# Queries and keys turned on the host, and a new order of small steps, in a bucketed-attention and expert kernel on one core

## The chip, the core and the metric

The program runs on one core of a Trainium2 chip. Its time is device microseconds of one execution, here the median of three timed runs. Engines: PE (matmul, with PEld its weight loads), DVE (vector), ACT (scalar), POOL (general), and SP, which here only issues DMAs.

## The reference

```python
# 2 batches, 8 heads, 768 tokens, head size 64; 6 hash bits
q_bits = (np.einsum('bhsd,dk->bhsk', q, proj) > 0)        # k_bits likewise
mask = q_bucket[:, :, :, None] == k_bucket[:, :, None, :]  # bits as one number
scores = np.where(mask, scale * q @ k.T, -1e9)
attn = softmax(scores); out = attn @ v
# then per token: argmax expert of 8 (w_gate), a 512-1024-512 relu layer, scaled by two gates
# then a dense 512-2048-512 layer with ELU
```

## The kernel before

The work has three stages: attention (to about 246 us of the profile), the experts, the dense layer. Only the first is touched.

Attention goes over 16 heads in 8 pairs; a pair is one q, one k and one v load. A tile is 128 queries of one head against its 768 keys; 6 tiles a head, 12 a pair, 96 in all. Every fp32 value is held as a high part (fp32r) and a low part (the rest), so that two single-speed products stand for one.

The loop `for n in range(NQ + 3)` writes a software pipeline out by hand. Iteration n issues, in this order: the maximum of tile n-1 (`stage_M`: DVE, then two tiny POOL instructions that make `sc` and `bi`), POOL additions (`stage_A`), work put off from the iteration before (`early`), the transposes of tile n-3 (`stage_T`: six on PE into two PSUM buffers; ACT copies each to the high part `pthi`, DVE subtracts for the low part `ptlo`), the scores of tile n (`stage_S`: four matmuls), the router product of an older head (`stage_R`), four matmuls with V for tiles further back (`stage_V`), the exponential of tile n-1 (`stage_E`, ACT), and the evacuation of finished outputs (`stage_O`). Scores have two PSUM buffers `s`, so the scores of tile n+1 wait for the exponential of tile n-1. Transposes, the hash product `zps` and the router product share three PSUM buffers `t`. All engines run in order; SP issues all operand moves in one queue.

While a pair is computed, the next one is prepared. Four steps (`prep_T`: q and k, two halves each) take three PE transposes of the raw rows, an ACT copy to the high part and a DVE subtraction to the low part; two steps (`prep_Z`) take four matmuls with the hash weights, an ACT copy and a DVE comparison. `late` spreads them over the tiles: the PE part stands at the end of iteration s = 1, 2, 4, 5 (transposes) and 7, 8 (hash) of a pair's twelve, its ACT and DVE part in the next iteration, the copy ahead of that iteration's scores and exponential. `restack` then has SP move the halves by DMA into operand tiles `qa`, `qb`, `ka`, `kb` of the two heads; there are two sets of operand tiles, for the even and the odd pairs. The scores are a product over 128 rows (`a`: high and low parts) and one over 102 rows (`b`: 64 rows of a low part and, from row 64 on, hash bits and constants).

Of the kernel before, what the change touches and what calls it, by code (L numbers as in the profile page):

```python
# [8 lines left out]
F32 = mybir.dt.float32  # L9
# [11 lines left out]
NBITS = 6  # L21
MROWS = 32 + NBITS


@with_exitstack
def kernel(
# [94 lines left out]
    def load_pair(pr, what="qkv"):  # L121
        b, h0 = divmod(2 * pr, H)
        for src, nm in ((q, "q"), (k, "k"), (v, "v")):
            if nm not in what:
                continue
            if nm == "v":
                t = ap2.tile([128, 2, NC * D], F32, tag="raw_v", name="raw_v")
                nc.sync.dma_start(t, src[b, h0:h0 + 2].rearrange("h (p c) d -> p h (c d)", c=NC))
            else:
                t = ap2.tile([128, NC, 2 * D], F32, tag="raw_" + nm, name="raw_" + nm, bufs=2 if nm == "q" else 1)  # L130
                step = HALF if pr == 0 else NC
                for c0 in range(0, NC, step):
                    for hh in range(2):
                        nc.sync.dma_start(
                            t[:, c0:c0 + step, hh * D:(hh + 1) * D],
                            src[b, h0 + hh].rearrange("(p c) d -> p c d", c=NC)[:, c0:c0 + step],
                        )
            raw[pr, nm] = t
# [24 lines left out]
    def constant_rows(st, parts):  # L163
        for i, c0, c1 in parts:
            nm, p0, n, a = (("qb", 64, 32, 0.0), ("qb", 96, NBITS, -0.5), ("kb", 64, 32, -0.5))[i]
            nc.gpsimd.memset(opnd[st, nm][p0:p0 + n, c0:c1].bitcast(F32), a)

    constant_rows(1, [(i, 0, S) for i in range(3)])
    constant_rows(2, [(i, 0, S) for i in range(2)])
    amp = ap1.tile([128, 1], F32, name="amp")  # L170
    thr = ap1.tile([128, 1], F32, name="thr")
    for p0, n, a, t in (
        (0, 32, 0.0, -3e38), (0, 2 * NBITS, 1.0, 0.0), (32, 32, -0.5, -3e38),
        (64, 32, -0.5, -3e38), (64, NBITS, 1.0, 0.0), (96, 32, 1.0, 0.0),
    ):
        nc.vector.memset(amp[p0:p0 + n], a)
        nc.vector.memset(thr[p0:p0 + n], t)
# [4 lines left out]
    for hh in range(2):  # L182
        rows = slice(64 * hh, 64 * hh + 64)
        src = pj[rows, None, :].to_broadcast([64, 2, NBITS])
        for nm, g0, c0, step in ((0, 32 * hh, 0, NBITS), (1, 64, NBITS * hh, 32)):
            dst = bdf[rows, nm, g0:g0 + 2 * step].rearrange("p (r c) -> p r c", r=2)[:, :, c0:c0 + NBITS]
            nc.scalar.activation(dst, src, AF.Copy)
# [16 lines left out]
    def prep_T(pr, nm, j):  # L204
# [3 lines left out]
        r = raw[pr, nm]  # L208
        ps = prep_psum("prep")
        for c in range(HALF):  # L210
            cc = HALF * j + c
            nc.tensor.transpose(ps[:, c * 128:(c + 1) * 128], r[:, cc, :], ident)
        sl = slice(j * HC, (j + 1) * HC)
        sc = 1.0 / float(D) ** 0.5 / UNIT

# [3 lines left out]
        def evac_lo():  # L219
            if nm == "q":  # L220
                nc.vector.scalar_tensor_tensor(lo[:, sl], ps, sc, hi[:, sl], ALU.mult, ALU.subtract)
            else:
                nc.vector.tensor_tensor(lo[:, sl], ps, hi[:, sl], ALU.subtract)
            if j == 1 and pr:
                restack(pr, nm)

# [36 lines left out]
    def bit_weights():  # L263
        nc.gpsimd.memset(zwf, 0.0)
        for hh in range(2):
            rows = slice(64 * hh, 64 * hh + 64)
            for i, c0, r in ((0, 2 * NBITS * hh, 2), (1, 32 + NBITS * hh, 1)):
                dst = zwf[rows, i, c0:c0 + r * NBITS].rearrange("p (r c) -> p r c", r=r)
                nc.gpsimd.tensor_copy(dst, pj[rows, None, :].to_broadcast([64, r, NBITS]))
        nc.gpsimd.tensor_copy(zw[:, :, 0:64], zwf)  # L270
        nc.gpsimd.tensor_tensor(zw[:, :, 64:128], zw[:, :, 0:64], zwf, ALU.subtract)

    def prep_Z(pr, j):
# [12 lines left out]
        def compare():  # L286
            nc.vector.tensor_tensor(zt[pr][0:64, sl], ps[0:64], zb, ALU.is_gt)
            if j == 1:
                restack(pr, "z")

        early.append(compare)
        return (lambda: None), (lambda: None)

    def restack(pr, what, heads=(0, 1)):
        for hh in heads:
# [87 lines left out]

    def stage_T(n, between=None):
        m, i = divmod(n, HALF)
# [6 lines left out]
        for g in range(2):  # L392
# [316 lines left out]
    for n, st, i in ((1, 2, 2), (2, 3, 0), (6, 3, 1), (7, 3, 2)):  # L709
        for j in range(2):  # L710
# [240 lines left out]
    for n in range(NQ + 3):  # L951
# [489 lines left out]
```

## Time and profile before

| | us |
|---|---|
| median of three timed runs | 712.71 (712.57 to 713.49) |
| the profiled execution | 713.77 |
| span of its instructions | 712.0 |

PE is busy 98% of the span, DVE 78%, ACT 60%, POOL 30%. The granted TensorE clock is 1.00 in every stretch of the attention stage. A busy PE is not a PE at its peak, since matmuls overlap and their ends are modelled, so the distances between starts are read below rather than the busy share.

### The profile page before, as it was taken

What the parts mean: (1) busy time and instruction counts of PE and PEld (TensorE: products, weight loads), DVE (VectorE), ACT (ScalarE), POOL (GpSimd) and SP (SyncE); (2) the same over time, 40 slices, a digit from 0 to 9 for tenths busy, and PEclk for the clock granted to TensorE, in tenths of its full rate; (3) what the DMA queues carried; (4) which work ended last, traced back from release to release, by engine and by line L of the source; (5) the groups of instructions that cost most, each with busy time, mean ns of one, the idle gap of its engine ahead of it and who ended that gap; (6) DMA issues with size and microseconds to landing.
All of it is one profiled execution on the core that took longest, in us unless ns stands there. A gap on an engine that the chain in (4) does not pass through costs nothing.

```text
span 712.0 us, 12226 instructions
## 1 busy us (share of the span) xinstructions
PE 698.5 (98%) x4211; PEld 626.8 (88%) x4212; DVE 553.7 (78%) x1046; ACT 428.4 (60%) x855; POOL 211.1 (30%) x508
## 2 busy tenths in 40 slices
PE   8999999999999999999999999999999999999996
PEld 6899999999998988999999998788888888888884
DVE  6989898899998997788888887877788547934433
ACT  6988888888888865666666665445443224422221
POOL 7665445455456661221065311000000000002012
PEclk9999999999999999999999999999999999999998
DMA  8857758686691239788878986322222000001011
GB/s 188 198 136 178 186 129 210 163 189 164 144 233 57 84 116 299 239 261 242 261 209 247 256 217 144 104 88 75 89 87 92 2 0 1 0 1 60 0 60 62
DMA packets 108596, 97.39 MB, mean 137 GB/s; under 512 B 33480, under 2 KB 94728, under 8 KB 108528
## 3 DMA queue, kind: packets, MB, share of 16 engines
q1 hardware_dynamic: 106064, 90.15, 47.3%
q0 software_dynamic: 2304, 6.40, 2.4%
q8 instruction: 35, 0.57, 0.3%
q14 instruction: 33, 0.27, 0.1%
q10 hardware_dynamic: 160, 0.00, 0.0%
HBM read 64.15 MB, written 10.72 MB: 105 GB/s over the span
## 4 chain that ended last, share of the span: by engine, by line
issue 32%; PE 23%; DMA 6%; POOL 1%; ACT 0%; SPq 0%; POOLq 0%; ACTq 0%
PE hps L1135 11%; PE yps L1148 7%; DMA out_dram<-part,tidt 5%; PE yps L1150 3%; DMA xs<-xs_d 1%; PE xTp L1117 1%; DMA tidt<-tid_d 1%; PE yps L1147 0%; POOL xs L857 0%; POOL out_dram L1293 0%; ACT sum L1153 0%; POOL spacer L612 0%; SPq L743 0%; POOLq L1293 0%; ACTq L1153 0%
## 5 line engine op out<-in xcount | busy, mean ns | idle before, releaser
L399 DVE TENSOR_TENSOR ptlo<-t,pthi 128x384 fp32r<-128x384 f32 x192 | 99.9, 548 | 14.7 <-ACT pthi L398 13.1
L376 ACT ACTIVATE p<-s,bi,sc 128x768 f32<-128x768 f32 x96 | 95.9, 999 | 17.5 <-POOL bi L369 15.7
L832 DVE TENSOR_TENSOR wl<-wraw,wh 128x1024 fp32r<-128x1024 f32 (+1 forms) x65 | 77.4, 1194 | 23.7 <-ACT wh L828 21.4
L367 DVE TENSOR_REDUCE nm<-s 128x1 f32<-128x768 f32 x96 | 90.9, 947 | 0.3 <-PE s L349 0.3
L398 ACT ACTIVATE pthi<-t 128x384 fp32r<-128x384 f32 x192 | 84.8, 497 | 10.2 <-PE t L396 8.9
L1293 POOL DMA_INDIRECT out_dram<-part,tidt x12 | 11.5, 960 | 263.5 <-DVE part L1290 262.2
L1255 ACT ACTIVATE ee<-gps 128x512 f32<-128x512 f32 x48 | 28.7, 597 | 98.0 <-PE gps L1245 98.0
L1148 PE MATMUL yps<-h,wh 128*128 128x448 f32 x256 | 84.4, 380 | 0.0
L396 PE MATMUL t<-ident,p 128*128 128x128 f32 x576 | 79.5, 273 | 0.0
L1245 PE MATMUL gps<-x2h,vl 128*128 128x512 f32 x192 | 75.9, 395 | 0.0
L1275 PE MATMUL a<-vh,gh 128*128 128x512 f32 x192 | 75.6, 394 | 0.0
L1275 PE MATMUL a<-vh,gl 128*128 128x512 f32 x192 | 75.4, 393 | 0.0
L1245 PE MATMUL gps<-x2h,vh 128*128 128x512 f32 x192 | 75.3, 392 | 0.0
L1245 PE MATMUL gps<-x2l,vh 128*128 128x512 f32 x192 | 75.2, 392 | 0.0
L1275 PE MATMUL a<-vl,gh 128*128 128x512 f32 x192 | 74.9, 390 | 0.0
L349 PE MATMUL s<-ka,qa 128*128 128x384 f32 x192 | 73.4, 383 | 1.2 <-DMA qa<-qlo 0.4
L1258 ACT ACTIVATE gh<-ee 128x512 fp32r<-128x512 f32 x48 | 30.4, 633 | 69.2 <-DVE ee L1257 69.2
L1256 DVE TENSOR_SCALAR ee<-ee 128x512 f32<-128x512 f32 x48 | 20.4, 426 | 66.3 <-ACT ee L1255 66.2
L396 PEld LDWEIGHTS t<-ident,p 128*128 128x128 f32 x576 | 67.4, 140 | 3.9 <-DVE ptlo L399 0.5
L828 ACT ACTIVATE wh<-wraw 128x1024 fp32r<-128x1024 f32 x63 | 66.2, 1052 | 2.7 <-DMA wraw<-in_moe_w_dram 2.7
L413 PE MATMUL o<-pthi,vst 128*128 128x384 f32 x192 | 66.9, 349 | 0.3
L349 PE MATMUL s<-kb,qb 102*128 102x384 f32 x192 | 65.3, 341 | 0.4 <-DMA kb<-z 0.4
(224 smaller groups left out, 1768.8 us busy)
## 6 DMA issues: line engine op xcount, KB each, us to landing
wraw<-in_moe_w_dram SPq DMA_DIRECT2D x64, 512.0 KB
w<-in_moe_w_in_dram SPq DMA_DIRECT2D x16, 512.0 KB
w<-in_moe_w_out_dram SPq DMA_DIRECT2D x16, 512.0 KB
ka<-khi SPq DMA_DIRECT2D x30, 192.0 KB
xs_d<-zt SPq DMA_DIRECT2D x8, 528.0 KB
xs<-xs_d SPq DMA_DIRECT2D x8, 528.0 KB
raw_v<-in_v_dram SPq DMA_DIRECT2D x8, 384.0 KB
kb<-klo SPq DMA_DIRECT2D x15, 192.0 KB
```

The lines of the kernel that those rows point to most:

```text
L349: nc.tensor.matmul(ps[:, j, 0:HC], opnd[st, "q" + x][0:n1, cb], opnd[st, "k" + x][0:n1, j * HC:(j + 1) * HC], start=(x == "a"), stop=(x == ...
L367: nc.vector.tensor_reduce(nm, sps[n][:, :, 0:HC], AX.XY, ALU.max, negate=True)
L376: nc.scalar.activation(p.rearrange("p (a b) -> p a b", a=2), sps.pop(n)[:, :, 0:HC], AF.Exp, bias=bi, scale=sc, accum_out=sums[hd][:, c:c ...
L396: nc.tensor.transpose(ps[:, a, :], p[:, kt * 128:(kt + 1) * 128], ident)
L398: nc.scalar.activation(ho, ps, AF.Copy)
L399: nc.vector.tensor_tensor(lo[:, HALF * g:HALF * (g + 1), i * 128:(i + 1) * 128], ps, ho, ALU.subtract)
L413: nc.tensor.matmul(ops[m], vst[hd][:, kt, :], t[:, kt, :], start=(kt == 0 and x == 0), stop=(kt == NC - 1 and x == 1))
L832: fs = [lambda c=slice(j, j + h): eng.tensor_tensor(lo[:, c], r[:, c], hi[:, c], ALU.subtract) for j in range(0, PW, h)]
L1135: nc.tensor.matmul(ps, w[:, dc, fs], x[:, dc], start=(i == 0), stop=(i == len(terms) - 1))
L1148: nc.tensor.matmul(ps, wh[:, f], h[:, :, f], start=(f == 0), stop=last)
L1245: nc.tensor.matmul(ps, w[:, dc], x[:, dc, th * TC:(th + 1) * TC], start=(dc == 0 and i == 0), stop=(dc == KD - 1 and i == 2),)
L1275: nc.tensor.matmul(ps, x[:, cs], w, start=(fb in first_fb and i == 0), stop=(fb in last_fb and i == 2))
```

## The change

The host hands over q and k a second time, laid out as [batch, head, 64, 768] with the tokens in the order in which the transposes left them (`q_t`, `k_t`). Pairs 1 to 7 load these, one DMA each, in place of two loads of 256-byte runs, and `prep_T` reads them from SBUF: no PE transposes and no PSUM buffer for 28 steps. Pair 0 is as it was.

The order changes too. In a tile's transposes the second of two low parts is issued in the next iteration, behind that iteration's maximum. The preparation's ACT copies stand behind the exponential, its subtractions an iteration later at `early`. The steps stand at other tiles of the pair that is computed meanwhile (one tile ahead of it, then s = 0, 3, 5; hash steps at 4 and 8). `stage_R` comes a tile later for all but the last twelve tiles. `restack` moves k and the hash bits head by head, and the bits in four moves a pair in place of six; the `b` product has 82 rows in place of 102, with the constants placed anew. The diff, cut to its core (the constants' memsets, weights' columns and the list of inputs are left out):

```diff
     def load_pair(pr, what="qkv"):
+            elif pr:
+                t = ap2.tile([128, S], F32, tag="raw_" + nm, name="raw_" + nm, bufs=2 if nm == "q" else 1)
+                src = q_t if nm == "q" else k_t
+                nc.sync.dma_start(t, src[b, h0:h0 + 2].rearrange("h d s -> (h d) s"))
...
     def prep_T(pr, nm, j):
-        ps = prep_psum("prep")
-        for c in range(HALF):
-            cc = HALF * j + c
-            nc.tensor.transpose(ps[:, c * 128:(c + 1) * 128], r[:, cc, :], ident)
         sl = slice(j * HC, (j + 1) * HC)
+        if pr:
+            ps = r[:, sl]
+        else:
+            ps = prep_psum("prep")
+            for c in range(HALF):
+                cc = HALF * j + c
+                nc.tensor.transpose(ps[:, c * 128:(c + 1) * 128], r[:, cc, :], ident)
...
             if j == 1 and pr:
-                restack(pr, nm)
+                restack(pr, nm, (0, 1) if nm == "q" else (0,))
...
     def prep_Z(pr, j):
...
             if j == 1:
-                restack(pr, "z")
+                restack(pr, "z", (0,))
+                restack(pr, "k", (1,))
+                restack(pr, "z", (1,))
...
     def restack(pr, what, heads=(0, 1)):
...
-                k0 = 32 + NBITS * hh if pr else 64 + NBITS * hh
-                cp("kb", 64, zt[pr], k0, NBITS)
-                cp("kb", 96, zt[pr], k0, NBITS)
-                cp("qb", 64, zt[pr], 2 * NBITS * hh if pr else 32 * hh, 2 * NBITS)
+                q0, k0 = (2 * NBITS * hh, 32 + 2 * NBITS * hh) if pr else (32, 96)
+                cp("qb", 64, zt[pr], q0, 2 * NBITS)
+                cp("kb", 64 + NBITS, zt[pr], k0, 2 * NBITS)
...
-    def stage_T(n, between=None):
+    lows_t = []
+
+    def stage_T(n, later, between=None):
...
-            nc.vector.tensor_tensor(lo[:, HALF * g:HALF * (g + 1), i * 128:(i + 1) * 128], ps, ho, ALU.subtract)
+            po = lo[:, HALF * g:HALF * (g + 1), i * 128:(i + 1) * 128]
+            if g and later:
+                lows_t.append(lambda: nc.vector.tensor_tensor(po, ps, ho, ALU.subtract))
+            else:
+                nc.vector.tensor_tensor(po, ps, ho, ALU.subtract)
...
-    def prep(pr, i):
-        return prep_T(pr, "qqkk"[i], i % 2) if i < 4 else prep_Z(pr, i - 4)
+    highs = []
+
+    def prep(pr, nm, j):
+        high, low = prep_T(pr, nm, j)
+        highs.append(high)
+        early.append(lambda: early.append(low))
...
+    for p in range(1, NPAIR):
+        n0 = 2 * NC * (p - 1)
+        for n, nm, j in (
+            ((2, "q", 0), (3, "q", 1), (4, "k", 0), (5, "k", 1)) if p == 1
+            else ((-1, "q", 0), (0, "k", 0), (3, "q", 1), (5, "k", 1))
+        ):
+            at(n0 + n, prep, p, nm, j)
+        for j, n in enumerate((7, 8) if p == 1 else (4, 8)):
+            at(n0 + n, prep_Z, p, j)
...
         if 1 <= n < NQ + 1:
             stage_M(n - 1)
+        both(lows_t)
+        lows_t.clear()
         stage_A(n)
...
-        if late:
-            late[0]()
...
-        m, part = divmod(n - 13, HALF)
+        m, part = divmod(n - (14 if n < NQ - 12 else 13), HALF)
         if 0 <= m < NM - 3 and part == 0:
             early.append(stage_R(m))
...
         if 1 <= n < NQ + 1:
             stage_E(n - 1)
+        both(highs)
+        highs.clear()
...
-        if late:
-            late[1]()
-            late = []
...
+        if name.endswith("_t"):
+            a = inputs[name[:-2]]
+            b, h, t, d = a.shape
+            a = a.reshape(b, h, 128, t // 128, d).transpose(0, 1, 4, 3, 2).reshape(b, h, d, t)
```

DVE in pair 3's stretch, where pair 4 is prepared: `nm` is a tile's maximum, `ptlo` a low part of transposed weights, `qlo` and `klo` those of the next pair's preparation. Before:

```order
L399 TENSOR_TENSOR ptlo<-t,pthi 128x3x128 x2
L367 TENSOR_REDUCE nm<-s 128x1
L399 TENSOR_TENSOR ptlo<-t,pthi 128x3x128
L460 RECIPROCAL ri<-sm 128x3
L399 TENSOR_TENSOR ptlo<-t,pthi 128x3x128
L221 SCALAR_TENSOR_TENSOR qlo<-prep,qhi 128x384
L367 TENSOR_REDUCE nm<-s 128x1
L399 TENSOR_TENSOR ptlo<-t,pthi 128x3x128 x2
L221 SCALAR_TENSOR_TENSOR qlo<-prep,qhi 128x384
```

Now (L409 is the put-off second low part, L411 the first):

```order
L373 TENSOR_REDUCE nm<-s 128x1
L409 TENSOR_TENSOR ptlo<-t,pthi 128x3x128
L226 SCALAR_TENSOR_TENSOR qlo<-raw_q,qhi 128x384
L411 TENSOR_TENSOR ptlo<-t,pthi 128x3x128
L373 TENSOR_REDUCE nm<-s 128x1
L409 TENSOR_TENSOR ptlo<-t,pthi 128x3x128
L228 TENSOR_TENSOR klo<-raw_k,khi 128x384
L411 TENSOR_TENSOR ptlo<-t,pthi 128x3x128
L472 RECIPROCAL ri<-sm 128x3
L373 TENSOR_REDUCE nm<-s 128x1
```

A maximum that stood behind both low parts and a preparation's subtraction now stands behind the first low part alone; the subtraction stands behind the maximum and reads `raw_q` or `raw_k`, where it read the PSUM tile `prep`.

SP, the end of pair 1's stretch, where pair 2's operands (head 0: `qa_128` to `kb_131`; head 1: `_132` to `_135`) and pair 3's raw rows are moved. Before:

```order
L134 DMA raw_q<-in_q_dram 128x6x64 x2
L134 DMA raw_k<-in_k_dram 128x6x64 x2
L443 DMA o_1082<-o_1081 64x384
L300 DMA kb_131<-z 6x768 x2
L300 DMA qb_129<-z 12x768
L300 DMA kb_135<-z 6x768 x2
L300 DMA qb_133<-z 12x768
```

Now:

```order
L134 DMA raw_q<-in_q_t_dram 128x768
L307 DMA ka_130<-khi 64x768 x2
L307 DMA kb_131<-klo 64x768
L455 DMA o_1026<-o_1025 64x384
L134 DMA raw_k<-in_k_t_dram 128x768
L307 DMA qb_129<-z 12x768
L307 DMA kb_131<-z 12x768
L307 DMA ka_134<-khi 64x768 x2
L307 DMA kb_135<-klo 64x768
L307 DMA qb_133<-z 12x768
L307 DMA kb_135<-z 12x768
```

Head 0's bits were behind both raw loads and both heads' keys; now they are behind one load of k in one piece, and head 1's keys follow them.

## Rows read from the trace of the kernel before

**Rows 1.** The page's first part: busy us, share, instructions.

```profile
PE 698.5 (98%) x4211; PEld 626.8 (88%) x4212; DVE 553.7 (78%) x1046; ACT 428.4 (60%) x855; POOL 211.1 (30%) x508
```

**Rows 2.** Windows of pair 3 and pair 7; stretch, length, busy by engine.

```profile
96.50:126.29 29.79, 29.79 (x204) 28.85 (x202) 26.85 (x51) 26.13 (x59) 14.80 (x46) 1.00 0.68 173
...
216.75:246.02 29.27, 28.81 (x189) 26.77 (x188) 26.17 (x52) 24.90 (x55) 18.05 (x48) 1.00 0.22 79
```

**Rows 3.** Windows of four tiles: plain, with transposes, hash, router.

```profile
119.26:121.33 2.07, 2.07 (x18) 2.03 (x15) 1.93 (x4) 2.00 (x6) 1.01 (x4) 1.00 0.94 189
130.80:133.20 2.40, 2.40 (x20) 2.36 (x19) 1.92 (x5) 2.40 (x6) 1.44 (x3) 1.00 0.12 43
116.48:119.26 2.78, 2.78 (x22) 2.74 (x20) 2.46 (x5) 2.72 (x7) 0.91 (x3) 1.00 1.02 224
121.33:124.22 2.89, 2.89 (x24) 2.85 (x22) 2.89 (x6) 1.96 (x5) 1.70 (x7) 1.00 0.50 121
```

**Rows 4.** PE's timeline: start, length, instruction, at a preparation's transposes.

```profile
129.90 0.49 PE L212 MATMUL prep<-ident,raw_q 128*128 128x128 f32 x3
130.22 0.82 PE L396 MATMUL t<-ident,p 128*128 128x128 f32 x6
```

**Rows 5.** The timeline of a plain tile, all engines.

```profile
126.82 1.02 DVE L399 TENSOR_TENSOR ptlo<-t,pthi 128x384 fp32r<-128x384 f32 x2 [0.18 <-ACT pthi L398]
126.90 0.34 PE L349 MATMUL s<-kb,qb 102*128 102x384 f32 x1
...
127.75 0.95 DVE L367 TENSOR_REDUCE nm<-s 128x1 f32<-128x768 f32 x1
...
129.18 0.19 POOL L369 TENSOR_TENSOR bi<-sc,nm 128x1 f32<-128x1 f32 x1
...
129.40 0.99 ACT L376 ACTIVATE p<-s,bi,sc 128x768 f32<-128x768 f32 x1 [0.22 <-DVE ptlo L399]
...
130.80 0.42 PE L349 MATMUL s<-ka,qa 128*128 128x384 f32 x1
```

**Rows 6.** Waits over the span: total us, times, longest.

```profile
PEld s L349 <- ACT p L376: 5.0, 18, 0.5
...
PEld prep L212 <- DVE ptlo L399: 0.8, 2, 0.5
...
PE s L349 <- DMA kb<-z: 0.4, 1, 0.4
```

**Rows 7.** Groups by line and form: copies and subtractions from PSUM and SBUF.

```profile
L1259 DVE TENSOR_TENSOR gl<-ee,gh 128x512 fp32r<-128x512 f32 x48 | 33.1, 689 | 14.3 <-ACT gh L1258 13.3
L1258 ACT ACTIVATE gh<-ee 128x512 fp32r<-128x512 f32 x48 | 30.4, 633 | 69.2 <-DVE ee L1257 69.2
...
L1290 DVE TENSOR_TENSOR part<-a,part 128x512 f32<-128x512 f32 x24 | 15.6, 682 | 3.0 <-PE a L1275 3.0
...
L1288 ACT ACTIVATE part<-a 128x512 f32<-128x512 f32 x12 | 6.2, 595 | 0.0
```

**Rows 8.** ACT's timeline in a tile with a preparation's copy.

```profile
130.75 0.87 ACT L398 ACTIVATE pthi<-t 128x384 fp32r<-128x384 f32 x2 [0.27 <-PE t L396]
131.51 0.50 ACT L217 ACTIVATE qhi<-prep 128x384 fp32r<-128x384 f32 x1
131.88 1.00 ACT L376 ACTIVATE p<-s,bi,sc 128x768 f32<-128x768 f32 x1
132.76 0.22 ACT L376 ACTIVATION_READ_ACCUMULATOR p<-s,bi,sc 128x1 f32 x1
```

**Rows 9.** The expert stage: line 857 in all, then POOL's and DVE's timeline.

```profile
L857 POOL TENSOR_SCALAR xs<-xs x16: 1556/1798/3191, 248.0 to 406.0; 128x512 f32<-128x512 f32 x16
...
292.06 4.94 POOL L857 TENSOR_SCALAR xs<-xs 128x512 f32<-128x512 f32 x2 [13.01 <-DMA xs<-xs_d]
...
291.75 1.22 DVE L832 TENSOR_TENSOR wl<-wraw,wh 128x1024 fp32r<-128x1024 f32 x1 [0.49 <-ACT wh L828]
...
294.43 1.23 DVE L832 TENSOR_TENSOR wl<-wraw,wh 128x1024 fp32r<-128x1024 f32 x1 [0.56 <-PE hps L1135]
```

More of the change, by code (lines that the diff above doesn't have):

```diff
@@ L21 @@
 NBITS = 6
-MROWS = 32 + NBITS
+MROWS = 3 * NBITS
 @with_exitstack
@@ L38 @@
     w_out: bass.AP,
+    q_t: bass.AP,
+    k_t: bass.AP,
     out: bass.AP,
@@ L128, in load_pair @@
                 nc.sync.dma_start(t, src[b, h0:h0 + 2].rearrange("h (p c) d -> p h (c d)", c=NC))
+            elif pr:
+                t = ap2.tile([128, S], F32, tag="raw_" + nm, name="raw_" + nm, bufs=2 if nm == "q" else 1)
+                src = q_t if nm == "q" else k_t
+                nc.sync.dma_start(t, src[b, h0:h0 + 2].rearrange("h d s -> (h d) s"))
             else:
                 t = ap2.tile([128, NC, 2 * D], F32, tag="raw_" + nm, name="raw_" + nm, bufs=2 if nm == "q" else 1)
-                step = HALF if pr == 0 else NC
-                for c0 in range(0, NC, step):
+                for c0 in range(0, NC, HALF):
                     for hh in range(2):
                         nc.sync.dma_start(
-                            t[:, c0:c0 + step, hh * D:(hh + 1) * D],
-                            src[b, h0 + hh].rearrange("(p c) d -> p c d", c=NC)[:, c0:c0 + step],
+                            t[:, c0:c0 + HALF, hh * D:(hh + 1) * D],
+                            src[b, h0 + hh].rearrange("(p c) d -> p c d", c=NC)[:, c0:c0 + HALF],
                         )
@@ L164, in constant_rows @@
         for i, c0, c1 in parts:
[L165 to L169, printed above, removed]
+            nc.gpsimd.memset(opnd[st, ("qb", "kb")[i]][64:96, c0:c1].bitcast(F32), -0.5)
+    constant_rows(1, [(i, 0, S) for i in range(2)])
     amp = ap1.tile([128, 1], F32, name="amp")
@@ L172 @@
     for p0, n, a, t in (
-        (0, 32, 0.0, -3e38), (0, 2 * NBITS, 1.0, 0.0), (32, 32, -0.5, -3e38),
-        (64, 32, -0.5, -3e38), (64, NBITS, 1.0, 0.0), (96, 32, 1.0, 0.0),
+        (0, 32, -0.5, -3e38), (0, 2 * NBITS, 1.0, 0.0), (64, 32, 1.0, 0.0), (64, NBITS, -0.5, -3e38),
     ):
@@ L184 @@
         src = pj[rows, None, :].to_broadcast([64, 2, NBITS])
-        for nm, g0, c0, step in ((0, 32 * hh, 0, NBITS), (1, 64, NBITS * hh, 32)):
-            dst = bdf[rows, nm, g0:g0 + 2 * step].rearrange("p (r c) -> p r c", r=2)[:, :, c0:c0 + NBITS]
+        for i, c0 in ((0, 32 * hh), (1, 64 + (32 if hh else NBITS))):
+            dst = bdf[rows, i, c0:c0 + 2 * NBITS].rearrange("p (r c) -> p r c", r=2)
             nc.scalar.activation(dst, src, AF.Copy)
@@ L266, in bit_weights @@
             rows = slice(64 * hh, 64 * hh + 64)
-            for i, c0, r in ((0, 2 * NBITS * hh, 2), (1, 32 + NBITS * hh, 1)):
-                dst = zwf[rows, i, c0:c0 + r * NBITS].rearrange("p (r c) -> p r c", r=r)
-                nc.gpsimd.tensor_copy(dst, pj[rows, None, :].to_broadcast([64, r, NBITS]))
+            for i in range(2):
+                c0 = 32 * i + 2 * NBITS * hh
+                dst = zwf[rows, i, c0:c0 + 2 * NBITS].rearrange("p (r c) -> p r c", r=2)
+                nc.gpsimd.tensor_copy(dst, pj[rows, None, :].to_broadcast([64, 2, NBITS]))
         nc.gpsimd.tensor_copy(zw[:, :, 0:64], zwf)
@@ L288, in compare @@
             if j == 1:
-                restack(pr, "z")
+                restack(pr, "z", (0,))
+                restack(pr, "k", (1,))
+                restack(pr, "z", (1,))
         early.append(compare)
-        return (lambda: None), (lambda: None)
     def restack(pr, what, heads=(0, 1)):
@@ L680 @@
     NM = 2 * NH
-    late, early = [], []
+    early = []
     v_at = (3, 5, 6, 8, 9, 11)
@@ L708 @@
             at(n, prep_V, p, i // 3, i % 3)
-    for n, st, i in ((1, 2, 2), (2, 3, 0), (6, 3, 1), (7, 3, 2)):
+    for n, st, i in ((1, 2, 0), (2, 2, 1), (6, 3, 0), (7, 3, 1)):
         for j in range(2):
@@ L957 @@
             stage_M(n - 1)
+        both(lows_t)
+        lows_t.clear()
         stage_A(n)
-        both(early)
-        early = []
+        now, early[:] = early[:], []
+        both(now)
         if 3 <= n < NQ + 3:
             m, part = divmod(n - 5, HALF)
-            stage_T(n - 3, (lambda: stage_G2(m)) if m >= 0 and part == 0 else None)
+            stage_T(n - 3, n < NQ, (lambda: stage_G2(m)) if m >= 0 and part == 0 else None)
         m, part = divmod(n - 4, HALF)
@@ L994 @@
         if nx < NPAIR:
-            i = s - 3 if pr == 0 else s // 3 * 2 + s % 3 - 1 if s % 3 else -1
-            if 0 <= i < 6:
-                late = prep(nx, i)
             if pr and s in v_at:
@@ L1002 @@
                 if s == 6:
-                    load_pair(nx + 1, "qk" if pr else "q")
-                elif s == 9 and pr == 0:
+                    load_pair(nx + 1, "q")
+                elif s == 8:
                     load_pair(nx + 1, "k")
@@ L1413 @@
 _INS = [
-    "q", "k", "v", "proj", "moe_w_gate", "moe_w_output_gate", "moe_w1", "moe_w2", "moe2_w_in", "moe2_w_out",
+    "q", "k", "v", "proj", "moe_w_gate", "moe_w_output_gate", "moe_w1", "moe_w2", "moe2_w_in", "moe2_w_out", "q_t", "k_t",
 ]
@@ L1428 @@
     for name in _INS:
-        a = _np.ascontiguousarray(inputs[name])
+        if name.endswith("_t"):
+            a = inputs[name[:-2]]
+            b, h, t, d = a.shape
+            a = a.reshape(b, h, 128, t // 128, d).transpose(0, 1, 4, 3, 2).reshape(b, h, d, t)
+        else:
+            a = inputs[name]
+        a = _np.ascontiguousarray(a)
         if a.dtype == _np.float64:
```

## The prediction

> **What bounds the kernel now.** I read the page first: PE is busy 98% of the span, far above DVE, ACT and POOL [rows 1]. That figure alone proves little, so I went to windows: one pair of tiles, then single tiles. In pair 3 (29.79 us) PE is busy throughout, while DVE and ACT are at 26.85 and 26.13 [rows 2]. Single tiles show what sets their length. A plain tile takes 2.07 us; one that also holds three preparation transposes takes 2.40 with two more loads of work on ACT, one with a hash step 2.78, one with a router product 2.89 [rows 3]. Length follows what PE has been given. Added up for a pair: 12 x 2.07 = 24.84, four transposing tiles 4 x 0.33 = 1.32, two hash steps 2 x 0.71 = 1.42, two router products 2 x 0.82 = 1.64, together 29.22. The pair took 29.79, so only about 0.57 us of it is waiting that comes on top. Attention is bound by PE's instruction stream, with the other three engines close behind.
>
> The second view is the cycle that would bound it next. In the timeline of a plain tile [rows 5] the scores end at 127.24 (126.90 + 0.34). The maximum starts only at 127.75, behind two low parts on DVE that took 1.02 us. POOL's `bi` starts 1.43 us after the maximum's start, the exponential at 129.40, and it ends at 130.39. It holds the buffer for the scores that PE starts at 130.80. Without the preparation between, PE would want that buffer 0.33 us sooner, at 130.47. The cycle has therefore some 0.08 us to spare as it stands, and the whole wait of scores for exponentials is 5.0 us in 18 cases [rows 6].
>
> **The change part by part.**
>
> The transposes. Three take 0.32 us of PE's stream: the preparation's begin at 129.90, the tile's own at 130.22 [rows 4]; the difference of the two tiles (0.33) says the same [rows 3]. Pairs 1 to 7 have four such steps each, 28 in all: 28 x 0.325 = 9.1 us off the stream that sets the length. What is late next is the cycle above, with 0.08 us to spare, and ACT.
>
> The second low part behind the maximum. Two low parts take 1.02 us and the maximum follows the first of them 0.93 later [rows 5], so one is about 0.47 us. With only one ahead of it, the maximum can start right at the scores' end, up to 0.51 us sooner. The cycle then has 0.59 us to spare in place of 0.08. The low part that is put off holds its PSUM buffer longer: maximum (0.95) and itself (0.55), to 1.5 us behind the scores. After a router product or a hash step the next transposes but one want that buffer; PE has by then done a V product (4 x 0.17) and the hash or router part (0.7 to 0.8) and half the transposes (0.33), 1.7 us or more, so that is hidden, by about 0.2 us. The gain is bounded by 0 and the 5.0 us that scores wait for exponentials now [rows 6]. I take 2.0: nearer to the row's half than to its whole, since ACT keeps some of it.
>
> ACT. The copies now read SBUF. No row shows 384 columns from SBUF; at 512 a copy is 633 ns from SBUF and 595 from PSUM, a subtraction 689 and 682 [rows 7]. That bounds the cost from both sides at 0 to 0.04 us per copy, on engines with idle time, and I count nothing. A tile with a copy needs on ACT 0.76 for two `pthi`, 0.37 for the copy, 0.88 for the exponential and some 0.1 for its accumulator [rows 8]: 2.11 us against PE's 2.07. The copies at s = 0 and 1 and the output's copy at s = 2 are three such tiles in a row, 0.12 us behind in all, within the 0.59. If that cover were gone, those 0.04 us per tile would be the cost.
>
> The preparation's subtraction against POOL. It had one operand in PSUM; now both lie in SBUF, and it stands 0.95 + 0.47 = 1.42 us behind the maximum's start, where `bi` starts on POOL at 1.43 [rows 5]. In the expert stage two POOL instructions that take 1.56 us at best took 4.94 together; DVE subtractions of two SBUF operands lay at 291.75 and 294.43, over the start of each [rows 9]: 1.8 us more than 2 x 1.56, the better part of 2 x 1.22. So I expect `bi` to be held while such a subtraction runs. The cost per subtraction is between 0 (`bi` goes first, or the 0.59 us covers it) and its whole 0.55 us: 0 to 28 x 0.55 = 15.4 us. I take 1.0, since 0.55 is just covered by 0.59 and only the tiles that are late already will show it. The Trainium skill (SBUF — State Buffer, section "SBUF: two separate sides") says that a DVE instruction with two SBUF inputs and a GpSimd instruction that reads SBUF lock each other out for a whole instruction. The expert stage's rows agree with it. By that rule alone, taken at every step, the sum would lose its upper end of 15.4 us, which is the slower rival below.
>
> The PSUM ring. The preparation's weight loads waited 0.8 us for a low part to free a buffer [rows 6]; 28 steps no longer take one. Bounds 0 and 0.8, and I take 0.5.
>
> SP and the moves. Scores waited 0.4 us for hash bits [rows 6]. Head 0's bits now stand behind one load of k in place of four raw loads, and in two moves in place of three. Bounds 0 and 0.4, and I take 0.4. Head 1's keys come later than they did, behind the bits of head 0; they are wanted three tiles (6 us) or more after head 0's, so nothing.
>
> The rest. The product of 82 rows streams the same columns as that of 102: nothing. The router product a tile later is the same PE work; its evacuation still lies beside V products: nothing either way, with the 0.57 us a pair of remaining waits as the bound. POOL loses a few memsets, at 30% busy: nothing.
>
> The sum, against the profiled execution's 713.77: -9.1 - 2.0 - 0.5 - 0.4 + 1.0 = -11.0, or 702.8. The experts and the dense layer follow as a block, because they start when attention ends and are bound by PE in their own right. The median before was 1.06 us below that profile, so the forecast of a median is 701.7.
>
> **The rivals.**
>
> Every wait goes. All of the 5.0, 0.8 and 0.4 us are won and `bi` is never held: 713.77 - 9.1 - 6.2 = 698.5, as a median 697.4. For it speaks that DVE and ACT have 3 us idle per pair [rows 2]; against it that pair 7, which prepares nothing and hence has the least on ACT, still takes 29.27 us with less PE work [rows 2].
>
> The cycle takes PE's place in part. If half of the 28 tiles stay near 2.40 us, because ACT (2.40 busy of 2.40 in such a tile [rows 3]) or a held `bi` sets them, 4.6 us come back, and of the 2.0 nothing is won: 713.77 - 9.1 + 4.6 - 0.9 + 1.0 = 710.4, median 709.3. Against it: ACT's busy share there includes waits for PE between the two `pthi`, and its own steps add up to 2.11.
>
> It does not do what it says to the time. All 28 tiles stay at 2.40 because exponentials pace them: 713.77 - 0.9, median 711.8, no change to speak of.
>
> Slower, by the lock on `bi`. If each of the 28 subtractions gets in ahead of `bi` and the 0.59 us is spent already, each costs 0.55: 713.77 - 9.1 - 0.9 + 15.4 = 719.2, median 718.1. It decides from 10.0 / 28 = 0.36 us exposed per subtraction on. For it: the two starts fall within 0.01 us of each other, and the expert stage shows the hold. Against it: it needs the maximum to gain nothing from its new place, and DVE has spare time in which the cycle recovers before the next.
>
> **How the numbers follow.** The forecast has 62%, everything won 11%, the partial case 16%, no change 6%, slower 5%. What a measurement of this kernel can tell from no change is about 0.2%, 1.4 us: from 711.3 to 714.1. Faster then has 62 + 11 + 15 = 88%, the same 7%, slower 5%. The forecast's own range is 699 to 705. For eight in ten I take 697.0 to 708.5: the lower end is the case in which everything is won, the upper lies just short of the partial case, so that a part of that one, no change and slower are left out.
>
> **What would show it.** Windows of pairs 2 to 6: about 28.2 us each, with some 12 fewer matmuls per pair. Tiles with a preparation: 2.07 to 2.15 us and not 2.40. In the timeline the maximum starts within 0.1 us of the scores' end. The wait of scores for exponentials is below 4 us in total. If `bi` is held, POOL's rows of line 369's operation are longer than 0.19 us or start more than 1.5 us behind the maximum, where a subtraction from `raw_q` or `raw_k` runs. I am wrong if the pairs stay near 29.8, if the expert stage gets longer, or if scores begin to wait for moves by DMA at the start of a pair.

## The result, and the profile after

The change took the median from 712.86 us (712.57 to 713.49) to 707.12 (706.88 to 708.05); the ratio on record is 0.9915, its 95% interval 0.9903 to 0.9928. That is faster by 5.7 us; the forecast was faster by 11.0. The profiled execution took 708.05 against 713.77, also 5.7 less. The span of its instructions fell by 6.8, from 712.0 to 705.2: 1.8 us of the time lay outside it before and 2.8 do after. No row shows what stands there; it is 1.8 to 2.5 us in the experiments below, so a part of a difference between kernels can come from there. The granted clock is 1.00 in every stretch of attention, as before, so the clock explains nothing.

PE's busy share did not move from 98% [rows 1], though 84 matmuls went:

```profile
PE 690.1 (98%) x4127; PEld 617.7 (88%) x4128; DVE 556.1 (79%) x1042; ACT 428.8 (61%) x855; POOL 217.1 (31%) x505
```

The share says nothing of where 5 us stayed. Windows by pair do (columns as in [rows 2]: stretch, length, busy by engine, clock, DMA share, GB/s). Of after, pairs 0, 1, 3, 5, 6:

```profile
9.31:36.72 27.41, 24.74 (x150) 21.14 (x147) 25.40 (x46) 22.88 (x49) 17.85 (x59) 1.00 0.82 210
36.72:65.00 28.28, 28.28 (x191) 27.41 (x189) 26.98 (x51) 26.13 (x59) 20.86 (x63) 1.00 0.62 147
93.23:121.50 28.27, 28.27 (x191) 27.46 (x190) 26.80 (x51) 26.14 (x59) 16.24 (x47) 1.00 0.70 181
149.99:180.10 30.11, 29.41 (x192) 27.36 (x189) 29.11 (x61) 26.66 (x62) 17.50 (x54) 1.00 0.68 174
180.10:211.44 31.34, 29.70 (x206) 27.66 (x204) 28.53 (x66) 27.10 (x61) 16.44 (x48) 1.00 0.67 175
```

And of before, pairs 0, 5, 6, which stood in no group ahead:

```profile
9.11:36.14 27.03, 25.60 (x161) 22.38 (x160) 25.30 (x46) 22.72 (x49) 16.43 (x58) 1.00 0.88 204
...
156.22:186.18 29.96, 29.89 (x203) 28.85 (x202) 27.73 (x61) 26.22 (x60) 15.37 (x51) 1.00 0.72 173
186.18:216.75 30.57, 30.45 (x218) 29.04 (x216) 28.00 (x66) 26.77 (x63) 15.43 (x49) 1.00 0.70 179
```

Pair 3 fell from 29.79 [rows 2] to 28.27. In pair 0 PE was already idle for 1.43 us before (27.03 - 25.60); after, its busy time is 0.86 less and its idle time 1.24 more (2.67). In pairs 5 and 6 PE was idle for 0.07 and 0.12 us before, and for 0.70 and 1.64 after. By pair, between the first scores of one pair and of the next (last tile's end for pair 7), in the profiled runs, the experiments' too:

| pair | before | after | e4 | e3 | e8 | e9 | e11 | e12 |
|---|---|---|---|---|---|---|---|---|
| 0 | 27.03 | 27.41 | 27.86 | 27.26 | 27.29 | 27.27 | 26.60 | 26.62 |
| 1 | 30.58 | 28.29 | 29.07 | 28.47 | 28.27 | 28.29 | 29.60 | 29.32 |
| 3 | 29.79 | 28.27 | 29.12 | 28.47 | 28.24 | 28.24 | 28.24 | 28.24 |
| 5 | 29.96 | 30.11 | 29.32 | 29.19 | 29.23 | 28.81 | 29.24 | 28.78 |
| 6 | 30.57 | 31.34 | 30.21 | 30.44 | 30.46 | 29.76 | 30.44 | 29.79 |
| 7 | 29.28 | 28.66 | 29.22 | 29.06 | 29.05 | 29.07 | 29.05 | 29.05 |

Pairs 2 and 4 go with pair 3 (before to after: 29.78 to 28.23, 29.93 to 28.48). So pairs 1 to 4 gave 6.8 us, pair 7 0.6, and pairs 0, 5 and 6 took 1.3 back. The stretch behind attention is 0.9 us shorter (466.0 to 465.1).

Single tiles of after, in the order of [rows 3]: two tiles that hold a preparation step, one with both a hash step and a router product, one with a router product, and the last tile of pair 6:

```profile
95.31:97.38 2.07, 2.07 (x17) 2.03 (x15) 2.07 (x5) 2.07 (x6) 0.98 (x3) 1.00 0.66 197
97.38:99.60 2.22, 2.22 (x17) 2.04 (x16) 2.22 (x6) 2.22 (x6) 1.77 (x3) 1.00 0.02 6
110.86:114.47 3.61, 3.61 (x27) 3.53 (x25) 3.08 (x8) 2.70 (x6) 2.64 (x8) 1.00 0.99 256
118.61:121.50 2.89, 2.89 (x23) 2.85 (x22) 2.81 (x7) 2.18 (x5) 2.01 (x6) 1.00 0.95 204
...
206.88:211.44 4.56, 3.50 (x31) 3.01 (x29) 2.86 (x8) 2.78 (x6) 1.88 (x6) 1.00 0.60 135
```

In pair 3 the tiles that took 2.40 take 2.07 to 2.22. Router and hash in one tile add up (2.07 + 0.71 + 0.82 = 3.60). The last tile does not: it has a router product and the gate's rank product, takes 4.56 where 3.23 was due (2.41 without the router product, measured in e8 below, and 0.82 for it), and PE is idle for 1.06 of it.

Waits of after over attention (total us, times, longest):

```profile
ACT p L382 <- POOL bi L375: 5.0, 10, 2.2
...
PEld s L355 <- ACT p L382: 3.5, 12, 0.5
...
DVE g_rk L570 <- PE sp L569: 1.8, 2, 1.6
PE t L404 <- DVE ptlo L409: 1.8, 5, 0.8
PEld t L404 <- DVE ptlo L411: 1.7, 3, 0.8
```

The first of PE's waits is that of [rows 6], down from 5.0. The last two rows are new in size: transposes wait for low parts, `L409` being the put-off one; the three cases of `L411` all lie in pair 0. PE's queue waits now for what the change has moved. In pairs 1 to 4 little is left: scores wait for exponentials there for 0.5 us in all.

### The profile page after: what moved, and what is told of

Same layout as the page of the kernel before. It is cut to its first block, busy times and chain, and to the rows that moved or that the text cites. A ratio compares the mean times of both kernels' runs of the same rounds, so it can differ in the third digit from the quotient of the medians.

```text
span 705.2 us, 12112 instructions
## 1 busy us (share of the span) xinstructions
PE 690.1 (98%) x4127; PEld 617.7 (88%) x4128; DVE 556.1 (79%) x1042; ACT 428.8 (61%) x855; POOL 217.1 (31%) x505
## 4 chain that ended last, share of the span: by engine, by line
PE 50%; issue 33%; DMA 6%; DVE 5%; ACT 2%; POOL 2%; SPq 0%; POOLq 0%; DVEq 0%; ACTq 0%
PE hps L1156 12%; PE yps L1169 7%; PE o L425 7%; PE s L355 7%; PE t L404 7%; DMA out_dram<-part,tidt 5%; PE yps L1171 3%; DVE nm L373 2%; PE sp L501 2%; PE zps L284 1%; PE xTp L1138 1%; ACT p L382 1%; DVE ptlo L411 1%; ACT pthi L406 1%; PE xacc L915 1%
## 5 line engine op out<-in xcount | busy, mean ns | idle before, releaser
L404 PE MATMUL t<-ident,p 128*128 128x128 f32 x576 | 81.2, 274 | 3.1 <-DVE ptlo L409 1.8
L355 PE MATMUL s<-kb,qb 82*128 82x384 f32 x192 | 65.1, 340 | 0.1
L425 PE MATMUL o<-ptlo,vst 128*128 128x384 f32 x192 | 65.0, 338 | 0.0
```

Source lines behind the costliest of these rows:

```text
L355: nc.tensor.matmul(ps[:, j, 0:HC], opnd[st, "q" + x][0:n1, cb], opnd[st, "k" + x][0:n1, j * HC:(j + 1) * HC], start=(x == "a"), stop=(x == ...
L404: nc.tensor.transpose(ps[:, a, :], p[:, kt * 128:(kt + 1) * 128], ident)
L425: nc.tensor.matmul(ops[m], vst[hd][:, kt, :], t[:, kt, :], start=(kt == 0 and x == 0), stop=(kt == NC - 1 and x == 1))
```

## The chain in the last tile of pair 6

The timeline of after, PE and DVE alone (start, length, instruction, idle time before it and what ended it):

```profile
207.67 0.98 PE L501 MATMUL sp<-rw,osb 128*128 128x160 f32 x6
...
209.31 0.22 PE L569 MATMUL sp<-cnt,ones_b 128*128 128x8 bf16 x3
...
209.57 0.18 DVE L570 TENSOR_TENSOR g_rk<-sp,ohs 128x24 f32<-128x24 f32 x1 [1.56 <-PE sp L569]
209.66 0.95 DVE L373 TENSOR_REDUCE nm<-s 128x1 f32<-128x768 f32 x1
...
209.80 0.55 PE L404 MATMUL t<-ident,p 128*128 128x128 f32 x3 [0.28 <-DVE g_rk L570]
...
210.53 0.55 DVE L409 TENSOR_TENSOR ptlo<-t,pthi 128x384 fp32r<-128x384 f32 x1
...
211.13 0.55 PE L404 MATMUL t<-ident,p 128*128 128x128 f32 x3 [0.78 <-DVE ptlo L409]
```

The gate of the experts runs in pairs 5 and 6; its rank product (`L569`, line 557 of before) and the router product (`L501`) both want one of the three buffers `t`. In the two pairs the rank product stands in two tiles only, the fourth and the last of pair 6. With the router a tile later it shares the last one with a router product. DVE reaches `g_rk` and sits for 1.56 us until the rank product, behind the router's 0.98 us on PE, is done. The maximum is queued behind `g_rk`, and the put-off low part behind the maximum. The scores it reduces had ended at 207.84; it starts at 209.66. The second half of the transposes needs the buffer that this low part frees, and waits 0.78 us. One late product is thus passed on three times.

Pair 5 has no rank product. What meets the later router product there are gate steps on DVE. In its ninth tile (168.28 to 172.68, 4.40 us; the tile with the same hash step and router product takes 3.61 in pair 3):

```profile
169.24 1.01 POOL L435 TENSOR_TENSOR osb<-o,o 64x384 f32<-64x384 f32 x1
169.48 0.82 DVE L586 TENSOR_TENSOR g_eq<-lg,g_mx 128x24 f32<-128x24 f32 x1
170.22 0.94 DVE L373 TENSOR_REDUCE nm<-s 128x1 f32<-128x768 f32 x1
...
171.78 1.15 PE L404 MATMUL t<-ident,p 128*128 128x128 f32 x6 [0.23 <-DVE ptlo L409]
```

The gate step `g_eq` ends with POOL's addition, the maximum behind it starts 0.97 us after its scores' end (169.25), and the transposes wait for the put-off low part. No run takes this one step away; e10 below moves all gate steps.

## The experiments

Two theories stood: A, the terms were right in kind and the missing gain is lost where the gate meets the new order; B, exponentials still pace the tiles, and the transposes leave PE for little. Ratios are against runs of before on the same chip. Those medians of before lie between 712.60 and 713.05, so a difference of less than 0.5 us between two experiments says nothing.

**e1, the turned q and k alone.** Before, with the new inputs and no transposes for pairs 1 to 7; order as it was.

```diff
-            ps = prep_psum("prep"); three transposes
+            ps = r[:, sl]   # pairs 1 to 7
```

> The order of the kernel before, with q and k turned by the host as the only edit: 28 x 3 transposes leave PE, all else stays. Theory (the order's other edits cost what the forecast missed, by low parts that are put off behind a maximum while DVE is behind): pairs 0, 5 and 6 are no longer than before, preparation tiles fall from 2.40 to about 2.1 us, 713.8 - 9.1 + some 1.5 of waits that come up = 705 to 706 in its profile, 1 to 2 us faster than the changed kernel. Rival (the new order is what lets the tiles fall, since the exponential's chain had only 0.08 us to spare): preparation tiles stay at 2.25 to 2.4 us, 709 to 712.

Measured 711.66, ratio 0.9980 (0.9971 to 0.9989): 1.3 us for 9.1 us of PE's stream. Its waits:

```profile
PEld s L358 <- ACT p L385: 13.4, 32, 0.9
...
PE s L358 <- ACT p L385: 5.1, 14, 0.6
```

The 5.0 us of [rows 6] became 13.4, and 5.1 more on the matmuls. What left PE came back as scores waiting for exponentials, as the rival had it.

**e2, no put-off.** The changed kernel with both low parts ahead of the next maximum.

```diff
-stage_T(n - 3, n < NQ, ...
+stage_T(n - 3, False, ...
```

> The changed kernel with both low parts of a tile ahead of the next maximum again. Theory (the put-off low part holds a transposes' buffer): the waits of transposes for low parts in pairs 0, 5 and 6 go, pairs 5 and 6 lose 0.8 us or more each, pair 0 about 0.8, pairs 1 to 4 gain 0.2 to 0.5 us each: 705 to 706.5. Rival 1 (the router product a tile later is what collides with the gate's steps and hash steps): pairs 5 and 6 stay at 30.1 and 31.3 us, time as the changed kernel or up to 2 us longer. Rival 2 (DVE is simply short of time beside the gate): all pairs longer by 0.5 us, 710.

Measured 712.99, ratio 0.9998 (0.9989 to 1.0007): the whole gain is gone, 5.9 us for a term put at 2.0, and more than any of the three forecasts had. The same wait:

```profile
PEld s L355 <- ACT p L382: 14.1, 41, 0.7
```

**e3 and e4, the router at its old tile, with the put-off and without.**

```diff
-divmod(n - (14 if n < NQ - 12 else 13), HALF)
+divmod(n - 13, HALF)
```

> The changed kernel with the router product at its old tile throughout. Theory of the put-off low part: only the tile that holds both the gate's rank product and a router product (4.55 us) recovers, 1 to 1.5 us: 705.7. Rival 1 (the router's tile is the cause): tiles 68, 71, 80 and 83, 4.40, 3.27, 4.01 and 4.55 us, go back to their 3.6, 2.9, 3.6 and 2.3 in sum with hash and router: 3 to 4 us faster, 703.5.

> Both undone, the put-off and the router's move. If the two causes are separate, the gains of the two single runs add (to about 0.5 us); if one is the cause of the other's loss, this is no better than the better of the two. Theory: 703.5 to 705. Rival 2 (DVE short of time): no better than the changed kernel's 707.

e3: 706.37 (0.9907, 0.9892 to 0.9922). e4: 709.13 (0.9944, 0.9930 to 0.9957). e3 is slower than both its forecasts, e4 than its theory, as its rival 2 had it. The router a tile later costs 0.75 us beside the put-off (the runs of after and e3 do not overlap, their intervals do) and 3.9 without it (e2). In e3 pairs 5 and 6 are 0.9 us shorter each than after, pair 3 0.2 longer: the later router helps where no gate runs and harms where one does. From e4 to e3 the put-off is worth 2.8 us. In e4 the wait of scores is

```profile
PEld s L355 <- ACT p L382: 10.5, 30, 0.7
```

and pair 3 is at 29.12: turned rows with the preparation's subtraction behind the maximum give 3.9 us without the put-off, not the 9.0 of the sum (-9.1 - 0.5 - 0.4 + 1.0). Without the put-off the exponentials pace the tiles, as theory B has it; with it they do not (3.5 us of wait in after), and theory A is left.

**e5, the put-off alone.** Before, with nothing but the second low part behind the next maximum.

```diff
-nc.vector.tensor_tensor(lo..., ps, ho, ALU.subtract)
+lows_t.append(...) if g and later else the same   # issued behind stage_M of the next iteration
```

> The kernel before with the put-off of the second low part as the only edit; the transposes stay on PE. Theory now (PE's stream and the exponential's chain each bound a tile, within 0.1 us of each other, so each edit alone gains little and both together gain): only the 0.57 us of waits per pair can go, pairs 2 to 5 at 29.2 to 29.6 us, 2 to 3 us in all: 710 to 711. Rival (the put-off is worth some 5 us by itself, as taking it out of the changed kernel cost): 707 to 708.

Measured 739.34, ratio 1.0379 (1.0361 to 1.0397): 26 us slower. Its largest wait of PE's matmuls, and its timeline at a preparation step:

```profile
PE t L398 <- DVE ptlo L403: 19.8, 29, 1.0
```

```profile
114.46 0.49 PE L212 MATMUL prep<-ident,raw_q 128*128 128x128 f32 x3
114.62 0.95 DVE L367 TENSOR_REDUCE nm<-s 128x1 f32<-128x768 f32 x1
...
115.48 0.55 DVE L403 TENSOR_TENSOR ptlo<-t,pthi 128x384 fp32r<-128x384 f32 x1
...
116.18 0.52 PE L398 MATMUL t<-ident,p 128*128 128x128 f32 x3 [0.88 <-DVE ptlo L403]
```

The preparation's transposes (`L212`) hold the third buffer, the put-off low part (`L403`) the second, and PE stands 0.88 us until DVE has done the maximum and then that low part. The put-off costs 26 us while the preparation's transposes use the ring of PSUM buffers, and 2.8 once the turned rows have left it (e1 to e6, next). Neither forecast of e5 saw that, and the prediction gave the ring 0.5 us.

**e6, turned rows and put-off, all else as before.** The edits of e1 and e5 together; the preparation's subtraction stays ahead of the next maximum:

```diff
+            ps = r[:, sl]                      # e1, pairs 1 to 7
+            if g and later: lows_t.append(...) # e5
```

> The kernel before with both: q and k turned by the host, and the put-off; steps, moves and router product stand where they stood. Theory: the gains do not add but multiply, pairs 2 to 4 near 28.4 us, pairs 5 and 6 about 0.9 us shorter than in the changed kernel, since the router product keeps its old tile: 705 to 707. Rival (the new places of the preparation's steps and its copies behind the exponential are needed too): pairs 2 to 4 at 29 us or more, 708.5 to 710.

Measured 714.44, ratio 1.0022 (1.0012 to 1.0031): slower than before, and slower than both forecasts; pairs 2 to 4 are at 29.9 to 30.0 us. Against e3 (8 us less) it lacks the new places of the preparation's copies, subtractions and PE steps, the new order of moves and the product of 82 rows.

**e7, the subtraction behind the tile's first low part.** The changed kernel, the preparation's subtraction moved to just ahead of the next maximum, away from `bi`.

```diff
-early.append(lambda: early.append(low))
+early.append(lambda: early.append(lambda: tail.append(low)))  # tail runs behind stage_T
```

> The changed kernel with the preparation's subtraction moved behind the first low part of the same iteration, so that it runs when POOL's bi is done. bi should go back from 0.50 to 0.57 us to 0.19 us in all 28 cases. Theory (the hold is covered by the room that the put-off made): no gain, and the next maximum is up to 0.4 us later at these tiles: 707 to 709. Rival (each held bi costs 0.1 to 0.2 us of scores' wait): 3 to 5 us faster, 702 to 704.

Measured 713.91, ratio 1.0014 (1.0003 to 1.0024): 6.8 us more than the changed kernel, where no forecast had a loss beyond 709. By line, `bi` in after, then `bi` and a subtraction in e7 (count, busy us, mean ns):

```profile
L375 POOL TENSOR_TENSOR bi<-sc,nm 128x1 f32<-128x1 f32 x96 | 27.5, 286 | 8.0
```

```profile
L375 POOL TENSOR_TENSOR bi<-sc,nm 128x1 f32<-128x1 f32 x96 | 18.4, 192 | 8.0
...
L228 DVE TENSOR_TENSOR klo<-raw_k,khi 128x384 fp32r<-128x384 f32 x14 | 11.5, 823 | 0.0
```

`bi` is free of the hold (192 ns, as before), and the time is worse: a subtraction ahead of the maximum costs far more than a held `bi`. Part of it may be that `klo` now takes 823 ns in place of 548, beside POOL's additions and subtractions; the two were not told apart.

**e8, the later router only where no gate runs.**

```diff
-14 if n < NQ - 12 else 13
+14 if n < 5 * 2 * NC else 13
```

> The changed kernel with the router product a tile later only up to tile 59, at its old tile from there on, where the gate's steps run. Theory (the later router product gains 0.2 us per pair in pairs 1 to 4 and meets the gate's rank product and DVE steps in pairs 5 and 6): pairs 1 to 4 at 28.2 to 28.5 as in the changed kernel, 5 and 6 at 29.2 and 30.4: 1.2 to 1.8 us faster than the changed kernel, 705.3 to 705.9. Rival (pairs 5 and 6 are slow by DVE's gate steps alone): 707.

Measured 705.47, ratio 0.9897 (0.9883 to 0.9911), 1.65 us less than the changed kernel; pairs 5 and 6 give 0.9 each. The last tile of pair 6, without the router product that now stands in the tile before it:

```profile
206.99:209.40 2.41, 2.41 (x24) 2.12 (x23) 1.35 (x5) 2.38 (x6) 0.96 (x2) 1.00 0.68 158
```

**e9, and no put-off where a router or hash product takes the third buffer.** e8, in pairs 5 and 6 only.

```diff
-stage_T(n - 3, n < NQ, ...
+stage_T(n - 3, n < NQ and not (60 <= n < 84 and n % 12 in (4, 7, 8, 10)), ...
```

> The split router order (old tile from n = 60 on), and in pairs 5 and 6 no second low part is put off in the four tiles of twelve (s = 4, 7, 8, 10) whose iteration or the next takes the third PSUM buffer t for a router or hash product. Theory: what is left above 28.3 us in these pairs is PE waiting for a buffer that a put-off low part holds; in the split order's tiles those waits are 0.43, 0.51 and 0.72 us, so with them gone the time falls by 1 to 1.5 us against that order (705.5): 704.0 to 704.7. Rival: in those tiles the maximum then stands behind a second low part, 0.47 us later, the exponential with it, and the gain is given back: 705.3 to 706.5.

Measured 704.42 (704.00 to 704.50), ratio 0.9880 (0.9865 to 0.9895). Pairs 5 and 6 lose 1.1 us more. The intervals of e8 and e9 overlap; the pairs of the table and the runs (704.00 to 704.50 against 705.03 to 706.02) tell them apart. The wait for the put-off low part has all but gone:

```profile
PE t L404 <- DVE ptlo L409: 0.3, 1, 0.3
```

**e10, the gate a tile later too.** The changed kernel, with

```diff
-def start(gi=2 * b + hf, n1=n0 + 8 * hf + 1):
+def start(gi=2 * b + hf, n1=n0 + 8 * hf + 2):
```

> The changed kernel with its router product a tile later throughout, and the gate steps of pairs 5 and 6 one tile later as well, so that router product and the gate's rank product stand to each other as before. Theory: pairs 5 and 6 lose because the moved router product falls into the tile of the gate's rank product; the loss goes as it did with the router at its old tile there: about 705.5. Rival: it is the gate's DVE steps beside the put-off low part, wherever the router stands: 706.8 to 707.5, pairs 5 and 6 at 30 and 31.3 us as in the changed kernel.

Measured 705.54, ratio 0.9894 (0.9879 to 0.9909), as the theory had it, but its reason holds for pair 6 at most. Pair 5 gains most, 1.4 us to 28.73, and has no rank product: what costs there is gate steps in the tiles of the later router product, on DVE as far as the trace shows it. Pair 6 falls to 30.85 only: its first rank product now meets a hash step (a tile of 4.46 us).

**e11, pair 1's preparation one tile later.** e8, with

```diff
-((2, "q", 0), (3, "q", 1), (4, "k", 0), (5, "k", 1)) if p == 1
+((3, "q", 0), (4, "q", 1), (5, "k", 0), (6, "k", 1)) if p == 1
```

> The split router order, and pair 1's four preparation steps one tile later each, at the tiles where they stood before (steps at 3 to 6 in place of 2 to 5). Theory: pair 0 took 27.3 to 27.4 us with the new places against 27.0 in the kernel before, whose steps stood there, so 0.3 us come back: 705.1. Rival: pair 0 is slower because its transposes wait for a put-off low part, whatever the places of the steps: 705.5, pair 0 at 27.3.

Measured 707.02, ratio 0.9918 (0.9905 to 0.9932). Neither forecast held. Pair 0 gave 0.7 us, and pair 1 lost 1.3 at its first scores:

```profile
37.23 0.41 PE L355 MATMUL s<-kb,qb 82*128 82x384 f32 x1 [1.09 <-DMA kb<-z]
```

SP had issued that move of hash bits by 32.8; it landed 4.4 us later, with pair 2's load of k, 384 KB, issued 2 us ahead of it in the same queue.

**e12, and pair 2's load of k behind those moves.** e9 with e11's steps, and

```diff
-elif s == 8:
+elif s == (8 if pr else 9):
     load_pair(nx + 1, "k")
```

> The kernel of the run on the third buffer (704.4), with pair 1's preparation steps at tiles 3 to 6, where they gave pair 0 0.7 us and cost pair 1 1.3, and pair 2's load of k one tile later in pair 0, so that it goes out behind the moves of pair 1's hash bits. Theory: the 1.3 us were scores waiting for bits that lay in the DMA queue behind 384 KB of loads; with the load behind them pair 1 is at 28.3 again and pair 0 keeps its 0.7: 703.5 to 704.0. Rival: the moves of q and k themselves are late, or the load now holds pair 2's first copy: pair 1 at 29 or more, 704.5 to 705.5.

Measured 703.54 (702.75 to 704.55), ratio 0.9865 (0.9848 to 0.9881). The time is that of the theory, the place that of the rival: the first scores of pair 1 no longer wait, but two tiles on `khi` starts late, a DVE subtraction behind it takes 1.32 us, and pair 1 stays at 29.32.

```profile
40.47 0.52 ACT L222 ACTIVATE khi<-raw_k 128x384 fp32r<-128x384 f32 x1 [0.45 <-issue]
...
41.03 1.32 DVE L228 TENSOR_TENSOR klo<-raw_k,khi 128x384 fp32r<-128x384 f32 x1 [0.37 <-ACT khi L222]
```

By pairs it is no shorter than e9, and the two intervals overlap: e9 and e12 both beat the changed kernel, and are not told apart.

## Why the prediction was half right

**The number.** The measured 707.12 lies in the range for eight in ten, 697.0 to 708.5, but outside the forecast's own, 699 to 705. It is in by the upper end alone, and that end owes something to luck: it was put just short of a partial case at 709.3, whose sum is wrong by 1.0. 713.77 - 9.1 + 4.6 - 0.9 + 1.0 is 709.4, as a median 708.3, inside the range and nearer to what was measured than the forecast of 701.7.

**The transposes, -9.1.** Right in pairs 1 to 4: their share of the whole sum was 11.0 x 4/7 = 6.3 us, and 6.8 were had. Wrong in pair 0: its four steps were counted at 0.325 each, though that pair was not bound by PE. The window of before shows 1.43 us of idle PE in it; it was not asked for, and pair 3 stood for all. There the forecast was -1.3 and +0.4 came: 1.7 us.

**The router a tile later, "nothing either way".** This step failed. In pairs 5 and 6 it costs 1.65 us (after against e8). In pair 6 the chain above is where: its last two tiles take 6.6 us in after and 5.3 in e8. In pair 5 the trace shows DVE's gate steps ahead of the maximum, and e10 agrees. In pairs 1 to 4 the move gains 0.2 each (e3). The bound named, 0.57 us of remaining waits a pair, was read in pair 3, where no gate runs.

**The put-off low part's hold on PSUM, "hidden, by about 0.2 us".** It is hidden in pairs 1 to 4. In pairs 5 and 6 the cover is gone, since gate steps stand in DVE's queue ahead of the low part: 1.1 us (e8 against e9). Together pairs 5 and 6 were forecast at -2.6 by their transposes and came at +0.9, 3.5 us short, of which e8 and e9 account for 2.9. With pair 0's 1.7 that is 5.2 of the 5.3 us missing. That the rest agrees is a sum of things no term stood for: pair 7 and the stretch behind attention came 1.5 us shorter, and 1.1 us more lies outside the span.

**The maximum, -2.0.** The mechanism was right, and the term measured 2.8 (e4 to e3); with the router a tile later it is 5.9 (e2 to after), above the bound of 5.0. That the terms add up was the deeper error: transposes alone -1.3, put-off alone +26, both with the old places +1.6, and with the new places -6.6 (e3). The sum came near in pairs 1 to 4 only because all its parts are there at once. The cycle of [rows 5] said so: 0.08 us to spare means that what leaves PE gains next to nothing until the exponential is sooner.

**The ring, -0.5, and the moves, -0.4.** Among PE's waits of after there is none of a preparation for a low part and none of scores for hash bits, so the waits of [rows 6] are gone. What the ring decides was missed: without its relief the put-off costs 26 us (e5).

**The lock on `bi`, +1.0.** The hold was seen and is covered. The timeline of after, at two preparation steps, and the end of a tile with none:

```profile
95.57 0.55 DVE L226 SCALAR_TENSOR_TENSOR qlo<-raw_q,qhi 128x384 fp32r<-128x384 f32 x1
95.67 0.50 POOL L375 TENSOR_TENSOR bi<-sc,nm 128x1 f32<-128x1 f32 x1
...
95.92 0.34 PE L355 MATMUL s<-kb,qb 82*128 82x384 f32 x1
96.04 0.55 DVE L411 TENSOR_TENSOR ptlo<-t,pthi 128x384 fp32r<-128x384 f32 x1
...
96.20 0.99 ACT L382 ACTIVATE p<-s,bi,sc 128x768 f32<-128x768 f32 x1
...
96.50 0.95 DVE L373 TENSOR_REDUCE nm<-s 128x1 f32<-128x768 f32 x1
...
97.38 0.42 PE L355 MATMUL s<-ka,qa 128*128 128x384 f32 x1
...
102.36 0.34 PE L355 MATMUL s<-kb,qb 82*128 82x384 f32 x1
...
102.79 0.96 DVE L373 TENSOR_REDUCE nm<-s 128x1 f32<-128x768 f32 x1
```

`bi` takes 0.50 us in place of 0.19 and ends as `qlo` does (96.17, 96.12). The exponential still ends at 97.19, 0.19 ahead of the scores that want its buffer. Over all 96, `bi` took 9.2 us more than 96 x 0.19, and hardly any of it reached PE in pairs 1 to 4, where scores wait 0.5 us for exponentials in all. The maximum starts 0.24 us behind the scores' end where a subtraction stands between and 0.09 where none does, against 0.51 before [rows 5]; 0.1 was forecast.

**ACT's copies.** Within the bounds of 0 to 0.04 us each. After has both kinds (count, busy us, mean ns):

```profile
L222 ACT ACTIVATE khi<-raw_k 128x384 fp32r<-128x384 f32 x14 | 7.4, 532 | 0.0
...
L222 ACT ACTIVATE khi<-prep 128x384 fp32r<-128x384 f32 x2 | 1.0, 492 | 0.7 <-PE prep L218 0.7
```

**The rivals.** None of them names the place. The partial case (709.3, rightly 708.3) had half the tiles slow everywhere; in fact all of them are fast in four pairs. The slower case needed the maximum to gain nothing, which is e7: there the time is above before, though with `bi` not held.

**What stays open.** In pair 0 PE's matmuls wait 0.9 us for the first low part `L411`, which stands behind a preparation's subtraction in DVE's queue; before, they waited for no low part there. In e11 that wait is 0.3 us and the pair 0.7 shorter, but no run changes it alone. Of the 8 us of e6 the place of the preparation's subtraction is likely the larger part, since e7, which changes only that place, costs 6.8; the other parts were not separated. What lies outside the span is not known.

## What to carry to other kernels

Where two chains are within 0.1 us of each other, do not price edits one by one: taking work from one is worth nothing until the other is shortened, and both may hang on a buffer that a third edit frees. Before a per-tile saving is multiplied by its count, read the idle time of that engine in every stretch that is counted, and look above all at the stretches with extra work. When an instruction moves by a tile, list what stands in the tile that it moves into, on every engine that waits in order.

## What the runs showed of the hardware

In 27 of the 28 cases of after, a DVE subtraction with two operands in SBUF lay over a `bi` on POOL, which took 0.39 to 0.58 us in place of 0.19 and ended 0.05 us behind the subtraction. In e7 it was the other way round: seven subtractions that started within a POOL addition of 1.01 us took 0.87 to 1.17 us in place of 0.55, and each ended 0.42 behind the addition. The Trainium skill (SBUF — State Buffer, section "SBUF: two separate sides") says that whichever of such a pair starts first keeps the port for its whole instruction; these rows agree with it. Subtractions whose operand is in PSUM showed no such hold in before, where `bi` never took more than 0.19 us.
